# Two score banks of one chunk for VectorE in a fused attention and GEGLU kernel

## The chip, the cores and the metric

The kernel runs on one core of a Trainium2 chip. The metric is the device time of one execution in microseconds (us); lower is better. Every timed comparison below alternates the two kernels on the same chip. "Clock" is the mean clock granted to TensorE in a run, 1 being full speed; a *position* is the number of a bank in the order of the 2048 banks of scores. Engines: PE is TensorE, ACT is ScalarE, DVE is VectorE, POOL is GpSimd.

## The reference

One transformer block on 2048 tokens of width 512, bf16:

```python
h = layernorm(x) * (1 + ca) + sa                # ca, sa, ga, cb, sb, gb come from silu(c) @ w_mod
x = x + ga * attention(h, wqkv, wo)             # 32 heads of 16, softmax over 2048 keys
h = layernorm(x) * (1 + cb) + sb
x = x + gb * (gelu(h @ w_gate) * (h @ w_up) @ w_down)     # 1792 wide
```

The softmax has 32 x 2048 x 2048 exponentials. In the kernel these are 2048 banks of 128 x 512 scores.

## The kernel before

The program is written by a greedy scheduler that runs while the kernel is built. It keeps a time for each engine and at every step records what it thinks can start next. The order is then fixed for each engine; between engines the program waits at semaphores.

The scores go through two halves of three PSUM banks. A chunk fills one half and is one exp instruction of ScalarE over two or three banks. VectorE can take a bank instead, with an approximate exp: a linear map into the bits of a bf16. It takes *rounds* of four banks, and each round is followed by three shifts in SBUF, on DVE or on POOL. A seventh bank (`mi`, the side bank) serves all other matmuls, the "side work": projections, output projection, feed-forward. If it is free, VectorE's bank goes there, and ScalarE still gets three.

```python
if len(mem) == CH and pos >= FIRST and not self.pressed() and self.free["dve"] + 600 < max(self.free["act"], t + 480) + 880 + LATE:
    ...                                    # cut: go on with the open round, or open a new one
gb = self.scp[:, s0 + CH - 1, :]           # the third score bank
if g is not None:
    for n in (CH, CH - 1):                 # first choice: three banks for ACT, side bank for DVE
        if n == CH and (self.open or (self.credit > SIDE and not idle)
                        or self.probe(lambda: self.mm(self.mi[:, 0:P], *filler)) > t + 30):
            continue
        mem, after = take(n)
        ...                                # cut
    if n == CH:
        gb = self.mi[:, :]
...
self.act(self.E[:, e0:e0 + n, :], self.scp[:, s0:s0 + n, :], ACT.Exp, scale=EXP_SCALE)
...
self.ts("dve", kq[:, 512 * j:512 * j + 512].bitcast(U16), gb, 128 / OCT, SHIFT_C, ALU.mult, ALU.add)
```

Queries come in six sets: three of 512 rows, one of 256 (set 3), two of 128 (sets 4 and 5). The side work of a set runs beside the exps of later sets. Sets 4 and 5 have none after them, so most of their feed-forward comes after the last exp.

The softmax here doesn't subtract the row's maximum and nothing guards it: scores larger than these inputs give would overflow.

Of the kernel before, what the change touches and what calls it, by code (L numbers as in the profile page):

```python
# [13 lines left out]
P = 128  # L14
# [24 lines left out]
CH = 3  # L39
# [17 lines left out]
SIDE = 1024  # L57
# [12 lines left out]
URGENT = 6  # L70
LAG = 40
SOLO = 2
SOON = 12
CLOSE = 48
BACK = 8
# [398 lines left out]
class _Kernel(_Recorder):  # L474
# [715 lines left out]
    def stream(self):  # L1190
# [25 lines left out]
        for u in units[2:]:  # L1216
            n, kpb = NKT * u[3] // 512, 512 // u[3]
# [9 lines left out]
        filler = self.filler = self.ident[:, :], self.xs[:, NT - 1, :]  # L1227
# [12 lines left out]
        quad = None  # L1240
# [3 lines left out]
        def take(n):  # L1244
            r, i = [], pos
            while len(r) < n and i < nseq:
                if i not in vec:
                    r.append(i)
                i += 1
            return r, i  # L1250
# [16 lines left out]
        def pv_next():  # L1267

            res = []
            for k in open_rounds():  # L1270
# [7 lines left out]
                if ("v", r * (512 // u[3]) // 4, u[1] // 2) not in self.have:  # L1278
                    if tq is not None and pos < SOON:
                        break  # L1280
# [45 lines left out]
        while cg <= group[units[-1]]:  # L1326
            t = max(self.pe_now(), virt)
            self.background(t)

            tq = None  # L1330
            mem, after = take(CH - 1 if pos < nsplit + 12 and c % 2 else CH)
            s0 = CH * (c % 2)
            if mem:
                e0 = 0 if e + len(mem) > NSL else e
                if all(owner.get(e0 + i, -1) < rp for i in range(len(mem))):
                    tq = self.probe(lambda: self.mm(self.scp[:, s0:s0 + CH, 0:P], *filler))
            if tq is not None and tq <= t + 30:
                slack = self.free["act"] - 600 - t
                w = self.next_side()
                if w is not None and pos >= w[1] and self.credit > 1536 and slack > 213 and self.probe(w[4][1]) <= t:  # L1340
                    self.advance()
                    continue
                short = self.short(t)
                if short > FILL - FLOOR or slack > 213 and short > 0:
                    self.mm(self.scp[:, s0, :], *filler)
                    continue
                g = None
                idle = w is None or self.probe(w[4][1]) > t + IDLE
                if len(mem) == CH and pos >= FIRST and not self.pressed() and self.free["dve"] + 600 < max(self.free["act"], t + 480) + 880 + LATE:
                    while quad is None and cand and rounds[cand[0]][2] < pos + (AHEAD1 if rounds[cand[0]][2] < nsplit else AHEAD):  # L1350
                        cand.pop(0)
                    if quad is not None:
                        g = quad["rnd"][2]
                    elif (cand and self.quad_free and (pos < ends[LATEK] or self.credit < CREDIT or idle) and rounds[cand[0]][2] < pos + 96 and self.backlog() < BACK
                          and all(k in self.have for k in self.keys(seq[rounds[cand[0]][2]]))):
                        rnd = rounds[cand.pop(0)]
                        quad = {"rnd": rnd, "j": list(range(4)), "k": self.quad_free.pop(0), "ready": [], "n": 4, "slots": {}, "used": set(range(4))}
                        left[rnd[0]] += 3
                        self.plain[rnd[0]] -= 1
                        g = rnd[2]  # L1360
                        vec.update(range(g, g + 4))
                        mem, after = take(CH)
                gb = self.scp[:, s0 + CH - 1, :]
                if g is not None:
                    for n in (CH, CH - 1):
                        if n == CH and (self.open or (self.credit > SIDE and not idle)
                                        or self.probe(lambda: self.mm(self.mi[:, 0:P], *filler)) > t + 30):
                            continue
                        mem, after = take(n)
                        js = [j for j in quad["j"] if j not in [seq[m][2] for m in mem]]  # L1370
                        if js:
                            break
                    if n == CH:
                        gb = self.mi[:, :]
                    j = (js or quad["j"])[0]
                    quad["j"].remove(j)
                    g += j
                items = [(m, self.scp[:, s0 + i, :]) for i, m in enumerate(mem)]
                if g is not None:
                    items.append((g, gb))  # L1380
                self.require(sorted({k for m, _ in items for k in self.keys(seq[m])}))
                self.qk([(seq[m], k) for m, k in items])
                n = len(mem)
                while self.step("act", self.free["act"]):
                    pass
                self.act(self.E[:, e0:e0 + n, :], self.scp[:, s0:s0 + n, :], ACT.Exp, scale=EXP_SCALE)
                for i, m in enumerate(mem):
                    owner[e0 + i] = rof[m]
                    self.slot[m] = self.E[:, e0 + i, :]
                if g is not None:  # L1390
                    kq = self.kq[quad["k"]]
                    while (self.free["dve"] + 1260 <= self.free["act"] + SLIP
                           and self.step("dve", max(self.free["dve"], t) + 40)):
                        pass
                    self.ts("dve", kq[:, 512 * j:512 * j + 512].bitcast(U16), gb, 128 / OCT, SHIFT_C,
                            ALU.mult, ALU.add)
                    if not quad["j"]:
                        quad["ready"].append((0, [kq[:, 512 * x:512 * x + 512] for x in range(4)]))
                        wait.append(quad)
                        for i in range(len(SHIFT)):  # L1400
                            self.shift_task(quad, i)
                        quad = None
                for w in self.work[:2]:
                    if pos >= w[1] and (w is self.work[0] or w[5]):
                        rate = w[3] / max(1, w[2] - pos)
                        self.credit = min(self.credit + rate * len(items), 4096)
                self.pos = pos = after
                e, c = e0 + n, c + 1
                continue
            gap = 1e9 if tq is None else tq - t  # L1410
            tp = pv_next()
            ok = [x[0] <= t + 30 for x in tp[:2]] + [False, False]
            w = self.next_side()
            ts = None
            side = False
            if w is not None and pos >= w[1]:
                ts = self.probe(w[4][1])
                n = w[4][0]
                side = (ts <= t + 30 and (self.credit >= n / 2 or (self.short(t) > 0 and self.credit > -2048))
                        and n / 2.4 <= gap + max(0, self.free["act"] - 600 - t - max(0, gap)))  # L1420
            hot = [x for x in tp if x[1] == 1 and x[0] <= t + 30] if len(self.sq_free) < HOT else []
            if hot:
                pv_do(hot[0])
                continue
            if ok[0] and (ok[1] or self.pe_mode == 2 or tq is None or not mem) and not (side and self.credit > 1536 and tq is not None and pos < nseq - CLOSE):
                pv_do(tp[0])
                continue
            if side:
                self.advance()
                continue  # L1430
            if ok[0] and gap > 400:
                pv_do(tp[0])
                continue
            nxt = [x for x in [tq, ts] + [x[0] for x in tp] if x is not None and x > t + 30]
            if self.tasks:
                nxt.append(max(self.free["dve"], t + 100))
            nxt = min(nxt) if nxt else t + 100
            if gap > 213 and not self.open and self.short(min(nxt, t + 1000)) > 0 and self.probe(
                    lambda: self.mm(self.mi[:, :], *filler)) <= t + 30:
                self.mm(self.mi[:, :], *filler)  # L1440
                continue
            virt = nxt
# [191 lines left out]
    def tail_ffn(self, ka, kb):  # L1634
# [49 lines left out]
        last, alone = None, []  # L1684
        for a in range(0, 4 * SOLO, 4):
            if ("t2", kb) in self.have:
# [54 lines left out]
```

## Time and profile before

| | before |
|---|---|
| time, three runs | 809.26 us median (807.15 to 809.9) |
| span of the profiled run | 806.9 us |
| busy: PE, DVE, ACT, POOL | 750.0, 671.3, 775.8, 277.4 us |
| exp banks on DVE / on ACT | 420 / 1628 |
| end of the last exp, and span after it | 780.0 us, 26.9 us |

Read it in two stages. Up to the last exp ScalarE sets the pace of the kernel, with almost no idle time (from 195 to 755 us it is busy 559.04 of 560 us). After it TensorE and a chain of small VectorE steps set the time (of the 26.9 us, 18.65 are TensorE's and 3.68 VectorE's in the chain that ended last). The prediction shows the lines of both.

### The profile page before, as it was taken

The numbers are of one execution on the slowest core, as the hardware profiler recorded it, in microseconds if no ns is written. First come the engines' busy times: TensorE is split into PE (matmuls) and PEld (weight loads), VectorE is DVE, ScalarE is ACT, GpSimd is POOL, SyncE is SP. The second block draws the span as 40 slices with busy tenths as digits, with TensorE's granted clock in tenths as the row PEclk, the third lists the DMA queues.
The fourth block names the chain that finished last, engine by engine and source line by source line (L and its number), as shares of the span: only waits on it lengthen the run. The fifth ranks groups of instructions, "written<-read, shape, count | busy, mean of one in ns | idle before, by whom it ended". The sixth has DMA issues, their size and how long they took to land.

```text
span 806.9 us, 27386 instructions
## 1 busy us (share of the span) xinstructions
PE 750.0 (93%) x12234; PEld 267.4 (33%) x12238; DVE 671.3 (83%) x1217; ACT 775.8 (96%) x732; POOL 277.4 (34%) x172
## 2 busy tenths in 40 slices
PE   8899999998899999999999899999999899999987
PEld 3334333322222222222222222222344342454455
DVE  6878898878898989988688998989778986677873
ACT  5999999999999999999999999999999999999982
POOL 3110335355545173356556346134262010000310
PEclk9999999999999999999999999999999999999999
DMA  9100000000022121111013111110123221120000
GB/s 312 55 9 19 10 10 16 10 16 10 16 55 67 35 54 36 48 41 29 24 24 110 36 52 51 48 42 16 41 62 87 64 73 39 33 76 13 22 9 15
DMA packets 58632, 36.03 MB, mean 45 GB/s; under 512 B 17977, under 2 KB 55090, under 8 KB 58514
## 3 DMA queue, kind: packets, MB, share of 16 engines
q1 hardware_dynamic: 56914, 32.84, 14.8%
q8 instruction: 96, 1.57, 0.8%
q10 hardware_dynamic: 1600, 1.44, 0.6%
q14 instruction: 22, 0.18, 0.1%
HBM read 29.62 MB, written 2.61 MB: 40 GB/s over the span
## 4 chain that ended last, share of the span: by engine, by line
ACT 86%; PE 9%; DVE 3%; DMA 1%; SPq 1%; issue 0%; DVEq 0%
ACT E L381 83%; PE ps_sc L368 4%; PE ps_mi L368 3%; ACT wreg L381 3%; PE ps_pv L368 1%; DVE mreg L393 1%; SPq L432 1%; DMA scr_rec<-rden 0%; DMA den<-scr_den 0%; DMA rb<-scr_rec 0%; DVE kmo L402 0%; DVE xs L385 0%; DVE dreg L393 0%; PE ps_mi L372 0%; DVE wreg L385 0%
## 5 line engine op out<-in xcount | busy, mean ns | idle before, releaser
L381 ACT ACTIVATE E<-ps_sc 128x1024 bf16<-128x1024 f32 (+2 forms) x686 | 749.0, 1282 | 16.7 <-PE ps_sc L368 16.1
L393 POOL TENSOR_SCALAR mreg<-dreg 128x2048 uint16<-128x2048 uint16 x93 | 175.0, 1898 | 261.9 <-DVE mreg L393 109.2
L393 DVE TENSOR_SCALAR dreg<-ps_sc 128x512 uint16<-128x512 f32 x253 | 171.7, 686 | 34.7 <-PE ps_sc L368 32.8
L368 PE MATMUL ps_sc<-qT,kme 32*128 32x512 bf16 (+2 forms) x1313 | 168.8, 333 | 18.7 <-ACT E L381 15.5
L368 PE MATMUL ps_sc<-qT,kmo 32*128 32x512 bf16 (+2 forms) x1313 | 173.7, 332 | 9.8 <-ACT E L381 8.6
L368 PE MATMUL ps_pv<-E,vaug 128*17 128x512 bf16 (+2 forms) x2112 | 150.6, 328 | 1.4 <-issue 0.9
L393 POOL TENSOR_SCALAR mreg<-mreg 128x2048 uint16<-128x2048 uint16 x46 | 86.5, 1898 | 139.5 <-DVE mreg L393 51.1
L368 PE MATMUL ps_pv<-mreg,vaug 128*17 128x512 bf16 (+2 forms) x1704 | 121.6, 337 | 1.7 <-DVE mreg L393 0.8
L393 DVE TENSOR_SCALAR mreg<-ps_sc 128x512 uint16<-128x512 f32 x126 | 85.5, 686 | 19.5 <-PE ps_sc L368 18.1
L368 PE MATMUL ps_mi<-wreg,mreg 128*32 128x512 bf16 (+1 forms) x1280 | 92.4, 372 | 4.4 <-DVE wreg L398 1.3
L368 PEld LDWEIGHTS ps_sc<-qT,kme 32*128 32x128 bf16 x1313 | 45.0, 91 | 145.2 <-ACT E L381 117.0
L368 PEld LDWEIGHTS ps_sc<-qT,kmo 32*128 32x128 bf16 x1313 | 45.7, 91 | 127.9 <-ACT E L381 108.9
L393 DVE TENSOR_SCALAR mreg<-dreg 128x2048 uint16<-128x2048 uint16 x117 | 76.9, 684 | 1.7 <-PE ps_pv L368 1.6
L368 PEld LDWEIGHTS ps_pv<-E,vaug 128*17 128x17 bf16 x2112 | 43.9, 89 | 62.2 <-issue 50.3
L368 PEld LDWEIGHTS ps_pv<-mreg,vaug 128*17 128x17 bf16 x1704 | 38.0, 89 | 36.6 <-issue 13.2
L402 DVE CAST wreg<-ps_mi 128x512 bf16<-128x512 f32 x49 | 33.6, 686 | 11.6 <-PE ps_mi L368 11.4
L368 PEld LDWEIGHTS ps_mi<-wreg,mreg 128*32 128x32 bf16 x1280 | 26.7, 95 | 44.0 <-issue 18.4
L368 PE MATMUL ps_mi<-hreg,wreg 128*32 128x512 bf16 x480 | 39.5, 384 | 0.0
L393 DVE TENSOR_SCALAR mreg<-mreg 128x2048 uint16<-128x2048 uint16 x59 | 38.4, 684 | 1.1 <-PE ps_pv L368 1.0
L398 DVE SCALAR_TENSOR_TENSOR wreg<-wreg,ps_mi 128x512 bf16<-128x512 bf16 x49 | 33.5, 683 | 6.5 <-PE ps_mi L368 5.0
L640 POOL TENSOR_SCALAR mv<-mv 128x4 f32<-128x4 f32 (+2 forms) x11 | 2.6, 240 | 94.8 <-DVE mv L425 93.9
L385 DVE TENSOR_TENSOR wreg<-wreg 128x1024 bf16<-128x1024 bf16 (+1 forms) x56 | 34.2, 618 | 0.5
(153 smaller groups left out, 672.6 us busy)
## 6 DMA issues: line engine op xcount, KB each, us to landing
mreg<-in_B_w_up_dram SPq DMA_DIRECT2D x22, 256.0 KB, 2.9
mreg<-in_B_w_gate_dram SPq DMA_DIRECT2D x15, 256.0 KB, 2.9
rb<-scr_rec SPq DMA_DIRECT2D x96, 32.0 KB, 1.8
dreg<-in_B_w_down_dram SPq DMA_DIRECT2D x9, 256.0 KB, 3.1
mreg<-in_w_mod_dram SPq DMA_DIRECT2D x1, 2048.0 KB, 13.3
mreg<-in_B_w_down_dram SPq DMA_DIRECT2D x8, 256.0 KB, 2.8
out_dram<-xs SPq DMA_DIRECT2D x16, 128.0 KB, 1.7
osb<-osb SPq DMA_DIRECT2D x48, 32.0 KB, 1.9
```

Source lines behind the costliest of these rows:

```text
L368: return self.rec("pe", lambda e: e.matmul(out, lhsT, rhs, start=start, stop=stop, tile_position=tp), [lhsT, rhs], [out], cost=(n, int(rhs ...
L381: return self.rec("act", lambda e: e.activation(out, in_, func, scale=scale, **kw), rd, wr, cost=self.cost("act", out, [in_], "act"))
L385: return self.rec(eng, lambda e: e.tensor_tensor(out, a, b, op), [a, b], [out], cost=self.cost(eng, out, [a, b], "tt"))
L393: return self.rec(eng, lambda e: e.tensor_scalar(out, a, s1, s2, **kw), rd, [out], cost=self.cost(eng, out, [a], "ts"))
L398: return self.rec("dve", lambda e: e.scalar_tensor_tensor(out, a, s, b, op0=op0, op1=op1), rd, [out], cost=self.cost("dve", out, [a, b], " ...
L402: return self.rec(eng, lambda e: e.tensor_copy(out, in_), [in_], [out], cost=self.cost(eng, out, [in_], "ts"))
L432: return e.dma_start(out, in_)
L640: self.rec("pool", lambda e: e.tensor_scalar(v, v, EPS, None, op0=ALU.add), [v], [v], cost=200)
```

## The change

Its intent: when VectorE is well ahead (320 ns) of ScalarE, let it take two banks of one chunk, the third score bank and the side bank.

```diff
+TWO = 320
...
+picks = []
 if g is not None:
-    for n in (CH, CH - 1):
-        if n == CH and (self.open or ...):
+    third, spare = self.scp[:, s0 + CH - 1, :], self.mi[:, :]
+    free = not (self.open or ...)                        # cut: the same condition as before
+    for banks in ((third, spare), (spare,), (third,)):
+        if not free and any(x is spare for x in banks):
             continue
-        mem, after = take(n)
+        if len(banks) == 2 and (len(quad["j"]) < 2 or self.free["dve"] + TWO > max(self.free["act"], t + 480)):
+            continue
+        mem, after = take(CH - any(x is third for x in banks))
         js = [j for j in quad["j"] if j not in [seq[m][2] for m in mem]]
-        if js:
+        if len(js) >= len(banks):
             break
-    ...
+    for gb in banks:
+        j = (js or quad["j"])[0]
+        ...                                              # cut: j and the bank go into picks
...
-if g is not None:
+for j, _, gb in picks:                                   # one DVE exp for each pick
```

With TWO so large that no pair is ever taken, the built program is the kernel before, instruction for instruction.

More of the change, by code (lines that the diff above doesn't have):

```diff
@@ L1362, in stream @@
                         mem, after = take(CH)
-                gb = self.scp[:, s0 + CH - 1, :]
+                picks = []
                 if g is not None:
-                    for n in (CH, CH - 1):
-                        if n == CH and (self.open or (self.credit > SIDE and not idle)
-                                        or self.probe(lambda: self.mm(self.mi[:, 0:P], *filler)) > t + 30):
+                    third, spare = self.scp[:, s0 + CH - 1, :], self.mi[:, :]
+                    free = not (self.open or (self.credit > SIDE and not idle)
+                                or self.probe(lambda: self.mm(self.mi[:, 0:P], *filler)) > t + 30)
+                    for banks in ((third, spare), (spare,), (third,)):
+                        if not free and any(x is spare for x in banks):
                             continue
-                        mem, after = take(n)
+                        if len(banks) == 2 and (len(quad["j"]) < 2 or self.free["dve"] + TWO > max(self.free["act"], t + 480)):
+                            continue
+                        mem, after = take(CH - any(x is third for x in banks))
                         js = [j for j in quad["j"] if j not in [seq[m][2] for m in mem]]
-                        if js:
+                        if len(js) >= len(banks):
                             break
-                    if n == CH:
-                        gb = self.mi[:, :]
-                    j = (js or quad["j"])[0]
-                    quad["j"].remove(j)
-                    g += j
+                    for gb in banks:
+                        j = (js or quad["j"])[0]
+                        quad["j"].remove(j)
+                        js = js[1:]
+                        picks.append((j, g + j, gb))
                 items = [(m, self.scp[:, s0 + i, :]) for i, m in enumerate(mem)]
-                if g is not None:
-                    items.append((g, gb))
+                items += [(m, gb) for _, m, gb in picks]
                 self.require(sorted({k for m, _ in items for k in self.keys(seq[m])}))
@@ L1389, in stream @@
                     self.slot[m] = self.E[:, e0 + i, :]
-                if g is not None:
+                for j, _, gb in picks:
                     kq = self.kq[quad["k"]]
@@ L1396, in stream @@
                             ALU.mult, ALU.add)
+                if picks:
                     if not quad["j"]:
```

## The prediction

> **What bounds the kernel now.** I read the page first (busy shares), then ScalarE's groups by shape, the table by stage, the chain that ended last, and at the end the timeline of the last 30 us.
>
> ```profile
> PE 750.0 (93%) x12234; PEld 267.4 (33%) x12238; DVE 671.3 (83%) x1217; ACT 775.8 (96%) x732; POOL 277.4 (34%) x172
> L381 ACT ACTIVATE E<-ps_sc 128x1024 bf16<-128x1024 f32 x407 | 399.7, 1120 | 1.2 <-PE ps_sc L368 1.1
> L381 ACT ACTIVATE E<-ps_sc 128x1536 bf16<-128x1536 f32 x271 | 391.6, 1544 | 3.1 <-PE ps_sc L368 2.6
> 195.00:755.00 560.00, 525.35 (x8141) 173.37 (x8142) 478.40 (x836) 559.04 (x517) 200.10 (x112) 1.00 0.17 46
> ```
>
> ScalarE (ACT) sets the pace. Its exps, on two score banks (1024 columns) or three (1536), take 791 us of the 806.9 us span and stand idle only 4.3 us before them. In the last line (a stretch of 560 us; busy time of PE, PEld, DVE, ACT, POOL) ACT is busy 559.04 us, 99.8%; VectorE (DVE) 478.40, 85%; TensorE 94%, of which a part is filler. So until the last exp the time is the sum of ScalarE's instructions, and a DVE exp is worth only what it takes off that sum.
>
> What one bank is worth I take from the chain, where ScalarE's starts follow each other without overlap (start, length, what):
>
> ```profile
> 454.96 0.92 ACT E L381
> 718.63 2.69 ACT E L381 x2
> ```
>
> A two-bank exp costs 0.92 us, a three-bank one 2.69 / 2 = 1.345 us. One bank less costs 0.425 us less, and a chunk (one exp instruction) keeps about 0.07 us of fixed cost.
>
> After the last exp ScalarE no longer matters. The chain then goes through TensorE and the feed-forward of the last two 128-row sets (set 4, set 5):
>
> ```profile
> 779.98 1.28 ACT L381 ACT_TABLE_LOAD   x1
> 781.38 1.49 ACT L381 ACTIVATE wreg<-ps_sc,modB 128x128 bf16<-128x128 bf16 x4
> 779.09 0.41 DVE L393 TENSOR_SCALAR hreg<-xs,mv,rstd 128x512 bf16<-128x512 bf16 x1 [1.08 <-POOL rstd L642]
> 780.86 1.77 DVE L405 RECIPROCAL rb<-ps_sc 128x128 f32<-128x128 f32 x2
> 782.81 0.57 PE L368 MATMUL ps_sc<-wreg,qT 128*128 128x128 bf16 x7
> 802.09 0.59 PE L368 MATMUL ps_mi<-dreg,hreg 128*128 128x512 bf16 x2
> ```
>
> Call L the end of the last exp, 779.96. Set 4's second layer norm (the third line) is done at 779.5, before L; so its modulate steps follow the table load at once (781.38), and the feed-forward's matmuls run in earnest from 782.81 = L + 2.85 to 802.6 = L + 22.6. Set 5's attention, projection and norm are hidden behind set 4's matmuls. From the last matmul to the end of the span is 4.3 us of scaling, adding and storing.
>
> [...] the trace has 686 ns for an exp bank of 512 columns and 684 ns for a shift of 2048 columns in SBUF, four times as many. [...] a shift is either 0.65 us of DVE or 1.9 us of POOL[...].
>
> **The change part by part.** It lets one chunk hand two banks to DVE: the third score bank and the side bank. I counted both built programs' instructions, and the chunks as the scheduler chose them.
>
> Chunks: 679 in both. Before, 379 chunks give the third bank and 41 the side bank. After, 369 give the third alone, 19 the side alone, 20 both. Banks on DVE: 379 + 41 = 420, then 369 + 19 + 40 = 428. So the 20 pairs mostly replace singles: rounds are picked for DVE four banks at a time, under conditions that the change leaves alone, and a pair finishes a round sooner rather than adding one. Only 2 rounds (105 to 107) are new.
>
> ScalarE: three-bank exps 271 to 262, two-bank 407 to 417, one single exp gone. 10 x 0.92 - 9 x 1.345 - 0.5 = -3.4 us, which is also 8 x 0.425. As ScalarE is 99.8% busy, all of it is on the path: L moves 3.4 us earlier.
>
> DVE: 8 exps x 0.686 = +5.5 us. Shifts: 315 to 321 in all, but the schedule also moves work from POOL: DVE's go from 176 to 199 (23 x 0.655 = +15.1 us), POOL's from 139 to 122 (17 x 1.88 = -32 us). DVE rises from 671 to about 692 us, 86% of the span. That is beside ScalarE, not on the path, as long as no bank comes free late.
>
> TensorE: two rounds need three more value passes each, 6 x 4 matmuls side by side at some 0.2 us, 1.3 us; filler matmuls drop from 96 to 76 in one group. Nothing on the path.
>
> The end: here the schedule changes more than the edit suggests. In the new order the last set-3 down-projection matmuls, which also need the side bank, still run among the last ten chunks, so set 4's output projection comes after the last score matmuls, where before 28 of these followed it. Set 4's norm now stands on DVE after both reciprocals and both products of set 5. I lay this out with the durations above, from L: value passes of the last chunk and the copy, to L + 0.95; statistics of set 4, 0.70 + 0.18, to 1.8; two reciprocals 1.77, to 3.6; two products 0.42, to 4.05; set 4's norm 0.41, to 4.5; transposes 0.4 and a semaphore, to 5.0; four modulate steps 1.49, to about 6.45. The feed-forward runs from L + 6.45, not L + 2.85. What it no longer has between its matmuls is part of set 5's projection (about 0.6 us). Its own matmuls are 112 x 0.109 + 28 x 0.215 = 18.2 us, with 0.25 of transposes and about 0.4 of gaps: end at L + 25.3 against L + 22.6. The built program agrees in kind: only one stage instead of two runs set 4 alone, and three fillers stand between the last exp and the feed-forward. The end is +2.7 us.
>
> Sum: -3.4 + 2.7 = -0.7. I add 0.5 us (my choice) for waits of ScalarE on a fuller DVE. 809.26 - 0.2 = 809.
>
> **The rivals.** (1) Every pair is a bank gained: 20 x 0.425 = -8.5 us, 801. For it: the intent. Against: 420 to 428 banks in the built program, which is no estimate. With the end unchanged the gain would be 3.4 us, 806. (2) DVE becomes the bound: in a pair chunk ScalarE takes 0.92 us and DVE 2 x 0.686 = 1.37 us, and DVE was already 94% busy in its fullest 50 us (300 to 350). If each of the 20 pairs held ScalarE for the 0.45 us difference: +9 us, 815. Against: a pair is allowed only if DVE is planned free 320 ns before ScalarE, a score bank has a second half to go to, and the third bank is read first; only the side bank comes free late, which delays side work, not exps. (3) Late side work lengthens the end, which is my main line; if it is hidden after all, 806, if set 4's projection slips further, 811. (4) POOL and DVE work moved about changes nothing: POOL is 34% busy.
>
> **Range and chances.** Everything lies between -3.4 and some +5 us; runs of the kernel before differ by 2.75 us by themselves. 804.5 to 813 holds the single terms with one of them off. 2% is 16 us, which no rival reaches: 0.02 for faster, 0.02 for slower.
>
> **What would show it.** Two-bank exps x417 and three-bank x262 are certain. Right: ScalarE's idle before exps still under about 6 us; last exp ending near 776.5; the first dense feed-forward matmuls some 6 us after it, no longer 2.85; DVE near 692 us busy. The ACT-sum step is wrong if ScalarE waits for scores by more than 3 us extra or the last exp does not move; the end step is wrong if the stretch from the last exp to the span's end stays at 27 us instead of about 29.7.

## The result, and the profile after

Ratios here are the mean time of one kernel's runs over that of the other's in the same rounds, so they are not quite the ratio of the medians quoted beside them.

The changed kernel took 807.27 us median (806.75 to 807.99, 4 runs), the kernel before 808.31 (807.15 to 809.9, 4 runs): ratio 0.9986, 95% interval 0.9964 to 1.0009. That is the same within 2%, and here not even clear of zero.

The lines of the kernel after that answer to the prediction's first fence: the page's busy times, the two shapes of ScalarE's exp (count, busy us, mean ns, idle before), and the stretch from 195 to 755 us (busy PE, PEld, DVE, ACT, POOL, granted clock).

```profile
PE 749.7 (93%) x12186; PEld 268.2 (33%) x12189; DVE 685.5 (85%) x1250; ACT 772.3 (96%) x732; POOL 245.8 (30%) x155
L382 ACT ACTIVATE E<-ps_sc 128x1024 bf16<-128x1024 f32 x417 | 409.7, 1111 | 0.9 <-PE ps_sc L369 0.9
L382 ACT ACTIVATE E<-ps_sc 128x1536 bf16<-128x1536 f32 x262 | 379.1, 1532 | 3.0 <-PE ps_sc L369 2.1 <-PE ps_mi L369 0.6
195.00:755.00 560.00, 523.59 (x8251) 175.87 (x8255) 494.69 (x871) 558.98 (x520) 176.34 (x99) 1.00 0.17 46
```

ScalarE is as full as before (558.98 of 560 us) and waits no more for scores (0.9 + 3.0 us against 1.2 + 3.1). Its two groups together lost 2.5 us of busy time. VectorE rose by 14 us, POOL fell by 32.

Now the end, in the timeline of the kernel after (start, length, what, idle before): ScalarE, VectorE, TensorE.

```profile
776.41 1.28 ACT L382 ACT_TABLE_LOAD   x1
780.92 1.51 ACT L382 ACTIVATE wreg<-ps_sc,modB 128x128 bf16<-128x128 bf16 x4 [3.01 <-PE ps_sc L373]
...
777.32 0.68 DVE L422 BATCH_NORM_STATS2 st<-xs 128x6 f32<-128x512 bf16 x1
778.14 1.74 DVE L406 RECIPROCAL rb<-ps_sc 128x128 f32<-128x128 f32 x2
779.79 0.42 DVE L386 TENSOR_TENSOR onormp<-osb,rb 128x128 bf16<-128x128 f32 x2
780.13 0.41 DVE L394 TENSOR_SCALAR hreg<-xs,mv,rstd 128x512 bf16<-128x512 bf16 x1
...
801.34 0.59 PE L369 MATMUL ps_mi<-dreg,hreg 128*128 128x512 bf16 x2
```

The last exp ends at 776.41, 3.57 us earlier than the 779.98 of before. But now ScalarE stands idle for 3.01 us after its table load: it waits for set 4's transposes, which wait for set 4's norm (780.13), and that comes behind two reciprocals and two products of set 5 on VectorE. In the kernel before this norm was done at 779.5, ahead of the last exp. In absolute time set 4 is hardly later than before: its rows are added from 776.18 us in the one and from 776.23 us in the other. The exps moved forward, and this step did not move with them. From the last exp to the span's end (806.2) it is 29.8 us, against 26.9. So -3.6 us and +2.9 us: the span is 0.7 us shorter. (Part of the 3.6 us is a disturbance in the one profiled run of the kernel before; see "Why the prediction was right".)

Where the lateness comes from shows in the stores of finished rows, one for each 128 rows, on the DMA-issuing queue. Set 3's two stores, in the kernel before:

```profile
748.90 0.36 SPq L432 DMA_DIRECT2D out_dram<-xs  x1
755.08 0.34 SPq L432 DMA_DIRECT2D out_dram<-xs  x1
```

and in the kernel after (the second line merges set 3's last store with the two at the end of the program):

```profile
762.23 0.34 SPq L433 DMA_DIRECT2D out_dram<-xs  x1
771.72 32.59 SPq L433 DMA_DIRECT2D out_dram<-xs  x3
```

Set 3's feed-forward is done at 755 before, at 772 after, though set 2's last store differs by only 2 us (711.85 and 709.70). Set 4's output projection comes after set 3 in the side work, hence after the last scores.

### The profile page after: what moved, and what is told of

The parts are those of the page before. It is cut to its first block, busy times and chain, and to the rows that moved or that the text cites. A ratio compares the mean times of both kernels' runs of the same rounds, so it can differ in the third digit from the quotient of the medians.

```text
span 806.2 us, 27296 instructions
## 1 busy us (share of the span) xinstructions
PE 749.7 (93%) x12186; PEld 268.2 (33%) x12189; DVE 685.5 (85%) x1250; ACT 772.3 (96%) x732; POOL 245.8 (30%) x155
## 4 chain that ended last, share of the span: by engine, by line
ACT 86%; PE 8%; DVE 4%; issue 0%; DMA 0%; SPq 0%; DVEq 0%
ACT E L382 83%; PE ps_sc L369 4%; PE ps_mi L369 3%; ACT wreg L382 3%; PE ps_pv L369 1%; DVE mreg L394 1%; DVE wreg L399 0%; DVE wreg L403 0%; DVE dreg L394 0%; DMA den<-scr_den 0%; DVE wreg L386 0%; SPq L433 0%; DVE kmo L403 0%; DVE rb L406 0%; DVE osb L403 0%
## 5 line engine op out<-in xcount | busy, mean ns | idle before, releaser
L394 POOL TENSOR_SCALAR mreg<-dreg 128x2048 uint16<-128x2048 uint16 x80 | 150.7, 1898 | 327.0 <-DVE mreg L394 180.2
L394 DVE TENSOR_SCALAR dreg<-ps_sc 128x512 uint16<-128x512 f32 x258 | 175.5, 686 | 33.0 <-PE ps_sc L369 31.0
L369 PE MATMUL ps_sc<-qT,kme 32*128 32x512 bf16 (+2 forms) x1316 | 174.7, 332 | 11.9 <-ACT E L382 8.6
L369 PE MATMUL ps_sc<-qT,kmo 32*128 32x512 bf16 (+2 forms) x1323 | 171.5, 331 | 13.4 <-ACT E L382 11.8
L394 POOL TENSOR_SCALAR mreg<-mreg 128x2048 uint16<-128x2048 uint16 x42 | 79.2, 1898 | 137.4 <-DVE mreg L394 85.5
L394 DVE TENSOR_SCALAR mreg<-ps_sc 128x512 uint16<-128x512 f32 x131 | 89.2, 686 | 17.8 <-PE ps_sc L369 15.6
L394 DVE TENSOR_SCALAR mreg<-dreg 128x2048 uint16<-128x2048 uint16 x133 | 87.6, 683 | 2.9 <-PE ps_pv L369 2.8
L394 DVE TENSOR_SCALAR mreg<-mreg 128x2048 uint16<-128x2048 uint16 x66 | 43.8, 684 | 1.7 <-PE ps_pv L369 1.7
L369 PE MATMUL ps_sc<-xs,ident 128*32 128x512 bf16 x304 | 25.6, 393 | 12.4 <-ACT E L382 12.1
```

The costliest lines, as they stand in the source:

```text
L369: return self.rec("pe", lambda e: e.matmul(out, lhsT, rhs, start=start, stop=stop, tile_position=tp), [lhsT, rhs], [out], cost=(n, int(rhs ...
L394: return self.rec(eng, lambda e: e.tensor_scalar(out, a, s1, s2, **kw), rd, [out], cost=self.cost(eng, out, [a], "ts"))
```

## The experiments

Theory: up to the last exp only the number of banks on VectorE counts (0.425 us each); after it only whether set 4's projection comes before or after the last scores. A pair as such does nothing; the edit changes these two numbers because it sends the scheduler on another course. (Both halves turn out too simple: a bank brings less than 0.425 us, and no_pairs_ahead24 and one_pair show that set 3's last rows can be what is late instead.) Rivals: a pair gives a bank each time; a pair holds ScalarE; the longer end has another cause.

The first table gathers what the profiled runs showed, each run a different program but for the repeat. "First to last exp" is from the start of ScalarE's first exp to the end of its last; it leaves out the start-up, which varies by 1.4 us from run to run (the first exp starts at 12.98 us in early_pairs_hold, at 14.37 in late_projection).

| kernel | pairs | DVE banks | first to last exp | span after it | ratio to before (95%) |
|---|---|---|---|---|---|
| before | 0 | 420 | 766.4 (one half-speed window) | 26.9 | 1 |
| after | 20 | 428 | 762.5 (one half-speed window) | 29.8 | 0.9986 (0.9964 to 1.0009) |
| after_again | 20 | 428 | 762.4 | 29.7 | 0.9991 (0.9978 to 1.0004) |
| late_projection | 0 | 420 | 764.5 | 30.9 (one half-speed window) | 1.0044 (1.0032 to 1.0056) |
| pairs_same_banks | 20 | 420 | 765.1 | 26.9 | 1.0015 (1.0001 to 1.0029) |
| early_pairs_hold | 3 | 428 | 765.6 (two half-speed windows) | 27.0 | 0.9986 (0.9974 to 0.9999) |
| pairs_anytime | 31 | 436 | 760.9 | 32.0 | 1.0044 (1.0022 to 1.0067) |
| no_pairs_ahead24 | 0 | 432 | 762.3 | 29.8 | 1.0000 (0.9988 to 1.0012) |
| one_pair | 1 | 432 | 762.2 | 34.0 | 1.0042 (1.0028 to 1.0055) |
| pairs_ahead22 | 22 | 432 | 763.2 (one half-speed window) | 26.9 | 0.9968 (0.9955 to 0.9982) |
| late400_no_pairs | 0 | 436 | 760.5 | 29.6 | 0.9987 (0.9970 to 1.0003) |
| late400 | 18 | 444 | 757.1 | 28.3 | 0.9931 (0.9916 to 0.9946) |
| late400_hold | 16 | 440 | 758.2 | 27.0 | 0.9912 (0.9898 to 0.9925) |
| pairs_same_banks_floor | 21 | 420 | 767.8 (one half-speed window) | 27.0 | 1.0030 (1.0016 to 1.0045) |

Half-speed windows are described below. The kernel before had a median of 807.2 to 807.6 us in the rounds of all the runs of this section.

**The repeat, after_again**, has no edit.

> The changed kernel once more, unaltered, with more rounds, because the first comparison (ratio 0.9986, 0.9964 to 1.0009) left open whether it is any faster. By the sum: span 0.7 us shorter, ratio 0.999; rival (no difference at all, or half-speed clock windows fall on it more often than on the kernel before): 1.000 or above, with runs at a mean clock of 0.993 to 0.995 some 2.5 us longer than those at 0.999.

Measured: 806.55 us (5 runs) against 807.61 (11 runs), ratio 0.9991. With the first comparison: the change is worth about 0.1% at most, in the direction that the sum gives, and neither interval excludes nothing at all. All five runs were at a mean clock of 0.999 or 1.000.

**The end alone, late_projection.** The kernel before; set 4's projection is held back to the last chunk.

```diff
-w.append((lambda: self.side_wo(k), s0, s0, True))
+w.append((lambda: self.side_wo(k), ends[-1] - 3, ends[-1] - 3, True))
```

> The kernel before with one edit: set 4's output projection may only be issued with the last chunk, so that it follows all score matmuls, as it does in the changed kernel. 420 banks on DVE, no pairs; the program is the same up to the last few chunks. My theory (the gain is given back at the end because set 4's projection comes late): the last exp ends where it did (about 780), the stretch from there to the span's end grows from 26.9 to about 29.8 us, and the time is 2.9 us above the kernel before (ratio about 1.0036). Rival (the longer end of the changed kernel comes from the pairs, or from DVE having more to do): no more than 0.5 us above the kernel before.

Measured: 811.11 us against 807.6, 3.5 us slower (2.9 expected). The timeline has the same picture as the changed kernel's end, without a pair and with 420 banks:

```profile
778.84 1.28 ACT L381 ACT_TABLE_LOAD   x1
783.62 1.50 ACT L381 ACTIVATE wreg<-ps_sc,modB 128x128 bf16<-128x128 bf16 x4 [3.29 <-PE ps_sc L372]
...
782.83 0.41 DVE L393 TENSOR_SCALAR hreg<-xs,mv,rstd 128x512 bf16<-128x512 bf16 x1
787.99 0.60 DVE L393 TENSOR_SCALAR wreg<-ps_sc,modB 128x128 bf16<-128x128 bf16 x2 [1.77 <-PE ps_sc L372]
```

The norm stands behind the reciprocals, ScalarE idles 3.29 us, and the end grows to 30.9 us. In this run TensorE had half its clock from 785.4 to 788.8, which is where VectorE waits 1.77 us in the last line (0.62 us in the changed kernel), so about 1.1 us of the 30.9 is that. The late projection alone gives the changed kernel's longer end. It does one thing more: from 765 us on, where the two runs part, the last exp gains about 0.8 us on the kernel before, probably because the last scores no longer queue behind set 4's projection. (Up to there the two have the same instructions on ScalarE and VectorE.)

**Pairs without banks, pairs_same_banks.** The changed kernel; no new round after position 1925 until set 3 is done.

```diff
-elif (cand and self.quad_free and (pos < ends[LATEK] or ...
+elif (cand and self.quad_free and not (pos >= 1925 and ('ffn', 3) not in self.have) and (pos < ends[LATEK] or ...
```

> The changed kernel, but no new round is opened for DVE after position 1925 while set 3's feed-forward is not finished. The built program has 20 pairs as the changed one, but 420 banks on DVE as the kernel before, and set 4's projection early again. My theory (only banks and the end count, a pair as such gives and costs nothing): the time of the kernel before, within 1 us; the last exp near 780, the end near 27 us. Rival (a pair as such is worth something, 0.425 us each): 5 to 8 us faster. Rival (a pair holds ScalarE 0.45 us): 9 us slower.

Measured: 808.74 us against 807.6. Twenty pairs, 420 banks, end 26.9 us. The six runs fall in two groups: 806.97, 807.52 and 807.86 at a mean clock of 0.999 or 1.000, and 809.61, 809.64 and 809.81 at 0.993 or 0.994. The first group takes as long as the kernel before. So a pair as such gives nothing and costs nothing measurable at full clock, both rivals fail, and the hold on new rounds brings the end back. The changed kernel shows the same in itself: built again with the choices printed, 17 of its 20 pairs come before position 1650, and at position 1800 (about 675 us) the traces of the kernel before and of the changed one have the same 392 banks on VectorE. All the extra banks come after that. The second group goes with a lower clock. That the pairs make such runs likelier is not shown: late400_no_pairs has them without a pair, and the nine runs of the changed kernel are all at 0.997 or above.

**A few early pairs, early_pairs_hold.** As above with 1900, and pairs only before position 700.

```diff
-if len(banks) == 2 and (len(quad["j"]) < 2 or ...
+if len(banks) == 2 and (pos >= 700 or len(quad["j"]) < 2 or ...
```

> The changed kernel with pairs allowed only before position 700 and no new round after 1900 while set 3's feed-forward is not finished. The built program has 3 pairs, 428 banks on DVE as the changed kernel, and set 4's projection early. My theory: the 3.4 us of ScalarE are kept whole: last exp near 776.5, end 26.9 us, 3.4 us below the kernel before (ratio 0.9958). Rival (the pairs make the gain): 3 pairs out of 20 give 0.5 us or nothing.

Measured: 806.4 us, ratio 0.9986, not the expected 0.9958. The end was 27.0 us as expected, but first to last exp took 765.6 us. TensorE had half clock twice in the profiled run (from 205.3 and from 730.9; the run's mean clock is 0.996), and ScalarE's waits there and soon after (206.82 to 737.44) add up to 2.3 us, with one of 0.77 us at 763.6. All six runs had a clock of 0.996 to 0.999. Taken alone this run doesn't decide, so pairs_ahead22 asked again.

**Pairs even when VectorE is late, pairs_anytime.**

```diff
-TWO = 320
+TWO = -2000
```

> The changed kernel with the condition on DVE's lead taken away (the margin of 320 ns set to -2000), so a pair is taken even when DVE is late. Built: 31 pairs, 436 banks on DVE, end late. Sum of ScalarE: 16 banks x 0.425 = -6.8 us at the last exp; the end about +3.5 us (an estimate from the scheduler's own plan, which had +1.7 where the chip gave +2.9, and has +2.7 here): 3 us below the kernel before. Rival (DVE as the bound: a pair taken while DVE is late holds ScalarE for up to 1.37 - 0.92 = 0.45 us and what DVE was late): last exp 5 us or more later than the sum says, idle before exps above 10 us before the end, time 3 us or more above the kernel before.

Measured: 810.73 us (807.13 to 813.42), 0.4% slower, where I had expected 3 us faster; by the time alone this is what the rival forecast. The profiled run, at full clock, took 807.82: first to last exp 760.9, about 4 us less than the 764.5 and 765.1 at 420 banks (the sum said 6.8), and an end of 32.0 us, 1.6 us longer than I had put it. But the rival's sign in the profile, over 10 us of idle time before exps, is absent: the waits of 0.16 us or more add up to 2.2 us after the first 80. The four longer runs (810.5 to 813.4) had a clock of 0.992 to 0.995 and were not profiled. So at full clock even 31 pairs without a condition don't make VectorE the bound; they lose about 3 us of the sum, and the long end takes the rest.

**Banks without pairs, no_pairs_ahead24 and late400_no_pairs.** Both are the kernel before with one constant changed.

```diff
-AHEAD = 20
+AHEAD = 24
```

> The kernel before with AHEAD 24 in place of 20 (a round is given to DVE only 24 positions ahead). Built: 432 banks, no pairs, set 4's projection late (end +3.1 us by the plan). Sum: -5.1 us at the last exp, end +3 to +5: time 0 to 2 us below the kernel before. It tests banks and end as two separate terms, without any pair: last exp near 774.9, stretch after it 30 to 32 us.

Measured: 808.15 us against 807.61. Last exp at 775.5 (expected 774.9), end 29.8 (expected 30 to 32), and the two cancel. But the end is not long for the reason that was expected. Set 4's projection is done before the last scores here, and its modulate steps follow the table load at once. What comes late is the down-projection of set 3's last rows (the third line), and behind it ScalarE waits 4.72 us, where some 2.0 are usual in this stretch:

```profile
775.47 1.28 ACT L381 ACT_TABLE_LOAD   x1
776.98 1.50 ACT L381 ACTIVATE wreg<-ps_sc,modB 128x128 bf16<-128x128 bf16 x4
789.09 1.46 PE L368 MATMUL ps_mi<-dreg,hreg 128*128 128x512 bf16 x6
793.28 0.60 ACT L381 ACTIVATE E<-ps_sc 128x512 bf16<-128x512 f32 x1 [4.72 <-PE ps_sc L368]
```

```diff
-LATE = 0
+LATE = 400
```

> The kernel before with LATE 400: the control without pairs. Built: 436 banks, no pairs, end +1.5 us by the scheduler's plan. Sum: 16 x 0.425 = -6.8 us, plus 2.5 for the end (plan scaled as for the changed kernel): 4 us below the kernel before. If the pairs are what makes late400 fast, this stays at the kernel before.

Measured: 806.74 us, 0.9 us less by the medians, where I expected 4. Last exp at 773.6, end 29.6. Three runs at 0.999 or 1.000 took 804.6 to 806.1, three at 0.994 or 0.995 took 807.4 to 808.8. Both kernels gain banks with no pair at all.

**One pair, one_pair.** The changed kernel with pairs only before position 520.

> The changed kernel with pairs allowed only before position 520: exactly one pair is left in the whole program. The program is the kernel before's up to that chunk; after it the scheduler goes another way: 432 banks on DVE in place of 420, and set 4's projection very late (the plan's end is 5.6 us longer). My theory (the edit acts by pushing the scheduler onto another course, not by what a pair does): last exp 4 to 5 us earlier, end 6 to 8 us longer, time 1 to 3 us above the kernel before. Rival (a pair acts by itself): one pair in 679 chunks changes less than 0.5 us.

Measured: 810.84 us against 807.61, 3.4 us slower by the ratio, a little more than expected. A single pair among 677 chunks, at one quarter of the stream (about 205 us), led to 432 banks and to an end of 34.0 us:

```profile
776.50 1.28 ACT L382 ACT_TABLE_LOAD   x1
...
784.90 0.60 ACT L382 ACTIVATE xs<-ps_sc 128x512 bf16<-128x512 f32 x1 [6.90 <-DVE E L394]
```

ScalarE idles 6.90 us after the table load: here even set 3's last rows are added after the last exp. One pair moved the time further than twenty did. What matters is the course that the scheduler takes. Set 4's projection is late here too, so how much of the 34.0 us is set 3's is not told apart.

**The gain kept, pairs_ahead22.** The changed kernel with AHEAD 22.

> The changed kernel with AHEAD 22 in place of 20. Built: 22 pairs, 432 banks on DVE, set 4's projection early. It asks whether the sum over ScalarE is kept where the end stays short, which early_pairs_hold left unclear because half-speed clock windows fell on it. Sum: 12 x 0.425 = -5.1 us from the first exp to the last, of which the earlier runs lost some 1 to 2.5 us to short waits; the end 27 to 27.3 us; time 2.5 to 4.5 us below the kernel before, ratio 0.9945 to 0.997 (less by 0.8 us for each half-speed window). Rival (the gain is lost also without a long end): ratio 0.999 or above with an end of 27 us.

Measured: 804.74 us against 807.19, ratio 0.9968. End 26.9 us, and the gain is there, 2.6 us of the sum's 5.1. In the profiled run, at a clock of 0.997, single waits of 1.57 and 0.78 us near 630 us took part of it; the two runs at a clock of 1.000 took 803.89 and 804.18.

**More banks, late400, and with the hold, late400_hold.** The changed kernel with LATE = 400; then also the hold at 1925.

> The changed kernel with LATE 400 in place of 0: a DVE bank may be taken though DVE is up to 400 ns later than before. Built: 444 banks on DVE, 18 pairs, set 4's projection rather early. Sum of ScalarE: 24 banks x 0.425 = -10.2 us; the end +1 us by the scheduler's plan; so 8 us below the kernel before (ratio 0.990), if ScalarE does not wait. Rival (DVE is by now the bound): ScalarE waits for scores several us more, time no better than the changed kernel.

Measured: 801.2 us against 807.61, ratio 0.9931: 5.6 us below the kernel before, where 8 were expected. Last exp at 770.2 (expected 769.8), end 28.3. The good fit of the last exp deceives: from the first exp to the last it is 7.7 us less than the 764.8 at 420 banks, not 10.2.

> late400 with the hold (no new round for DVE after position 1925 while set 3's feed-forward is not finished). Built: 440 banks, set 4's projection early. Sum: 20 x 0.425 = -8.5 us at the last exp, of which about 1.5 to 2 us are lost to waits as in late400; end 27 us: 6.5 us below the kernel before, about as late400, ratio 0.992.

Measured: 800.58 us (799.39 to 801.27) against 807.61, ratio 0.9912. The unaltered change took 806.55. The hold costs four banks, 1.1 us up to the last exp, and gives 1.3 us at the end. The end of this kernel:

```profile
771.39 1.28 ACT L382 ACT_TABLE_LOAD   x1
772.80 1.49 ACT L382 ACTIVATE wreg<-ps_sc,modB 128x128 bf16<-128x128 bf16 x4
...
195.00:755.00 560.00, 527.82 (x8415) 177.88 (x8411) 498.68 (x879) 559.40 (x526) 200.88 (x113) 1.00 0.17 47
```

Set 4's modulate steps follow the table load at once, as in the kernel before, and ScalarE is still 559.40 of 560 us busy with VectorE at 89%. This version beats both kernels. Whether it needs the pairs is not shown: the control without them has 436 banks and another end.

**The half-speed windows, pairs_same_banks_floor.** In some runs TensorE is granted half its clock for a few us; the two stretches whose ends I read, one in each profiled run of the first comparison, are 3.41 us long. In the kernel before it is the one from 248.01 to 251.42 us, the second of these two neighbouring stretches (the clock is the number after POOL's):

```profile
244.60:248.00 3.40, 2.12 (x31) 0.56 (x31) 2.87 (x8) 3.40 (x4) 1.27 (x2) 1.00 0.02 5
248.00:251.40 3.40, 3.40 (x30) 1.18 (x30) 2.30 (x5) 2.59 (x3) 0.95 (x1) 0.50 0.00 0
```

TensorE was busy only 2.12 of 3.40 us, and then ran at 0.50. ScalarE waited for scores in it:

```profile
249.56 1.02 ACT L381 ACTIVATE E<-ps_sc 128x1024 bf16<-128x1024 f32 x1 [0.32 <-PE ps_sc L368]
251.08 1.45 ACT L381 ACTIVATE E<-ps_sc 128x1536 bf16<-128x1536 f32 x1 [0.49 <-PE ps_sc L368]
```

That is 0.8 us of waiting. Against late_projection, which has the same exps and no window there, the kernel before falls behind by 1.1 us in these few chunks. The window itself takes away half of 3.41 us, 1.7 us of clock, so not all of it reaches the exps. The two groups of pairs_same_banks show the same: at mean clocks of 0.9933 and 0.9993 they differ by 0.006 x 807 = 4.8 us of lost clock, but only by 2.2 us of time. A kernel may meet a window in one run and miss it in the next: the changed kernel's profiled run has one from 426.2 us, its repeat none before the last exp. How empty TensorE was does not tell by itself where a window comes. In that profiled run it was busy 2.48 of 3.40 us before the window, and only 2.17 of 3.40 us from 221.4 us, where none followed. I tried to close the windows with more forced fillers, on my guess that more work on TensorE keeps them away:

```diff
-FLOOR = 3300
+FLOOR = 3700
```

> pairs_same_banks with FLOOR 3700 in place of 3300: fillers are forced on TensorE at a higher activity. Built: 420 banks, early projection, 33 pairs-or-side banks, last exp planned 1 us later. In pairs_same_banks half of the runs had a mean granted clock of 0.993 and were 2.3 us longer than those at 0.999. If those half-speed windows come from stretches of too little TensorE work, here all runs stay at 0.997 or above and within 1.5 us of each other. If not, the two groups of runs appear again.

Measured: 810.3 us (808.87 to 811.0), ratio 1.0030. No run was below 0.997 and the two groups are gone, but the spread is 2.1 us, one window still fell in the profiled run (from 449.6, with ScalarE waiting 1.09 us at 453.59), and first to last exp is 2.6 us longer than in pairs_same_banks. The scheduler also placed everything else differently, so this is inconclusive on what sets the windows off, and no remedy.

## Why the prediction was right

- **The bound.** Right in kind: ScalarE stayed 99.8% busy, and the last exp came earlier. That its 3.57 us in the profiled runs meet the 3.4 predicted is partly luck. About 1.1 us of it is the half-speed window of the kernel before, and about 0.8 us is what the late projection gives the last chunks by itself, as in late_projection; a start-up longer by 0.3 us goes the other way. Against late_projection (420 banks, projection late, no window before the last exp) first to last exp is shorter by 2.1 us, against pairs_same_banks (420 banks, projection early, no window) by 2.7. So eight banks were worth some 2 to 2.7 us, not 3.4. The table shows the same: from 420 to 444 banks first to last exp falls from about 764.8 to 757.1, 0.32 us a bank instead of 0.425. Idle time before exps grew by 1.2 to 1.6 us of the 2.5 us missing there (4.6 us in late400, 3.0 in late_projection, 3.4 in pairs_same_banks); what took the rest is not shown.
- **The pairs mostly replace singles.** Right: 428 banks, 20 pairs. pairs_same_banks and one_pair go further than I had: the number of pairs does not set the number of banks at all.
- **VectorE and POOL.** The work was right (rows of the profile: 22 us more by VectorE's groups, 20.6 predicted), the busy time was off: 685.5 us, not 692, since neighbouring instructions overlap (the norm at 780.13 us in the timeline above starts while the products run to 780.21) and busy time counts an overlap once: VectorE's groups add up to 720.5 us before and 742.5 after, its busy time is 671.3 and 685.5. POOL fell by 32 us as predicted.
- **The end.** Right step by step: norm of set 4 at L + 4.1 (4.5 predicted), end of modulate and dense feed-forward from L + 6.0 (6.45), last matmul at L + 25.5 (25.3), span after the last exp 29.8 (29.7). late_projection shows the cause by itself, for this kernel; in others of the table another piece of side work is late.
- **Waits on a fuller VectorE, +0.5 us.** Not seen at that size: idle time before exps went from 4.3 to 3.9 us, with a window in both runs; without one it is 3.0 us (late_projection) and 3.4 us (after_again). Without this term the difference is -0.7 us, and the measured ones are -1.1 and -0.7 us (0.14% and 0.09%). This fit should not be trusted: from the first exp to the end of the span the changed kernel took 792.2 us in both its profiled runs, and the kernel before 793.3, which is also about 792.2 without its window.
- **The level.** The 809.0 is 1.7 us above the 807.27 measured. Most of that is the starting point: the first three runs of the kernel before had a median of 809.26, all later rounds 807.2 to 807.6.
- **The rivals.** "Every pair is a bank gained" and "a pair holds ScalarE" both fail in pairs_same_banks. The prediction's third, that the late side work lengthens the end, is what happened.

What was argued and not shown on its own is why set 3's feed-forward runs late in the changed kernel. From 712 to 755 us VectorE was busy 37.63 us against 32.97 before, and the hold on new rounds cures it, so VectorE's rounds there are involved; whether they delay it by VectorE's time, by the side bank or by the shorter chunks of ScalarE, no run tells apart.

## What to carry to other kernels

Before crediting an offload, count in the built program how much of the bound engine's work really goes away; here a rule that fires twenty times removed eight banks. When a greedy scheduler writes the program, a small edit reshuffles everything after it, so judge it by the sum of the bound engine and by the stretch after its last instruction, each measured, and protect that last stretch explicitly. Look at the granted clock of each run before explaining a difference of 2 us: in pairs_same_banks the runs at 0.993 took 2.2 us longer than those at 0.999.
